# Later marks, sooner routing, and rows mixed by a copy and turned in one pass, in a fused attention and MoE kernel

## The chip, the cores and the metric

The kernel runs on one core of one Trainium2 chip. The metric is the device time of one execution in microseconds; of several executions the median stands.

## What is computed

Three stages follow each other. The first is sliding-window attention over 4 sequences of 576 tokens with 8 heads of 64 (window 64); its output is a matrix x of 2304 rows and 512 columns. The second is a mixture of 8 experts, of which each row takes the two with the highest noisy logits. The third is an MLP with a squared gate.

```python
scores = scale * np.matmul(q, k.transpose(0, 1, 3, 2))
mask = (rel >= 0) & (rel < window)
...
noisy_logits = logits + noise_scale * noise
top2 = np.argpartition(-noisy_logits, 2, axis=1)[:, :2]
...
for e in range(E):
    for k in range(2):
        mask = top2[:, k] == e
        h = np.maximum(x[mask] @ w1[e], 0.0)
        out[mask] += top2_w[mask, k, None] * (h @ w2[e])
...
h = x @ w_in
g = np.where(pos, h, np.where(neg, 0.0, (h + beta) ** 2 / (4.0 * beta)))
return (g @ w_out).astype(np.float32)
```

All data are float32. The kernel forms the large products from a high part (f32r, the value rounded by a copy) and a low part (value minus high part), in three products: high by high, high by low, low by high.

## The kernel before

One function writes the program of all engines in the order of its Python code, and each engine runs its own instructions in that order. SyncE (SP) issues most loads and stores; GpSimd (POOL) issues gathers and scatters by index.

**Attention.** Steps u = 0 to 36 go over half-tiles of 64 rows. Each step issues scores, exponentials and products of several half-tiles at different stages (top, soft, C, Dm, Ex). Dm scales a finished tile of x on VectorE (DVE: rl, its reciprocal, a multiplication) and stores it to x_dram. In the same steps the weights of the first expert come in: load_raw loads a chunk of 128 hidden columns, split_w makes its high part on ScalarE (ACT, L158) and rest_w its low part on DVE (L149); there are seven such chunks (EW) in the attention and one more behind it.

**Routing.** The 18 tiles of x are routed in three groups of 8, 4 and 6 tiles. `route(g)` is a generator: its pieces are some twenty small DVE operations (m, t, uu, w, ny, MAX8 and MAX_INDEX for the two best experts, then ohs, the one-hot marks) and two on ACT (y, L). Then PE counts, for each row, its place among the rows of its expert (L558 to L562, bank<-ohs), and DVE makes marks (ohr, ohe) from which `place` (L634) adds up row numbers on PE. `advance` and `tail`/`more` issue the next pieces; `early` gathers the first three blocks of rows of expert 0, for the unit 0a, before the third group is routed.

**MoE.** Units 0a, 0b, e1 to e6, 7a and 7b are blocks of rows of one expert. For each of eight chunks n, `do_mm1(n)` makes twelve products (L891) and the activation (ACT L899, DVE L902: hall), and `do_mm2` the products with the second weights (L964). In the code do_mm1 runs one chunk ahead of do_mm2.

**The second MLP.** Unit g0 (two blocks of 128 rows) is computed plainly. Units g1 to g4 (four blocks each) use the Strassen-Winograd scheme: for each of eight rounds p, `wino` makes seven products of six matmuls each (L1178) in seven slots j, which alternate between two banks of PSUM; DVE and ACT combine them into cg (L1163, L1168; an eviction frees the bank for the product two slots later). The gate (L1196 to L1206) turns cg into hall, and mm2 matmuls (L964) of an earlier round fill the slots between the products.

During a unit the next one is prepared. Each row of the MoE's output is a weighted sum of two gathered rows y1 and y2 (`prep_mix`: two scalings on ACT, L1043 and L1044, and an addition on POOL, L1045). `xturn` turns it by four transposes on PE (L1236), `xcopy` copies it to xf on ACT (L1242), `xsums` makes four differences xd of quarter matrices (L1255; on POOL, for the first Winograd unit on DVE), and `xsplit` high and low parts. The slot (p, j) of each step is written in the main loop and in the table AT.

## Time and profile before

| | |
|---|---|
| median of 3 runs | 954.07 us (952.11 to 954.48) |
| profiled execution | 953.95 us, span 952.2 us |
| mean granted clock of PE | 0.998 |
| PE busy | 938.4 us |
| DVE busy | 659.5 us |
| ACT busy | 444.3 us |
| POOL busy | 222.1 us |

The span goes from the first to the last instruction of the profiled execution; 1.75 us of its time lie outside. An engine is busy while one of its instructions is under way, whatever the clock of PE is. The granted clock is the share of full speed that the throttle leaves to PE. In a timeline a row gives start and duration in us, engine, line, operation, out<-in with partitions and elements, how many alike are joined in it (x9), and in brackets how long the engine was idle before and what ended that.

### The profile page before, as it was taken

To read this page: it belongs to the slowest core of one execution; us is meant where nothing else is said; L and a number is where in the kernel's file an instruction comes from. 1 tells how busy PE (TensorE), PEld (TensorE's weight loads), DVE (VectorE), ACT (ScalarE), POOL (GpSimd) and SP (SyncE) were. 2 spreads that over 40 slices of the span, in tenths; PEclk is the share of its full clock that TensorE was granted. 3 is DMA by queue.
4 is the path that set the end of the run, shared out by engine and by line. 5 is a ranking of instruction groups with operands and counts; after the bars stand their busy time and mean duration, and the time that the engine had idled before them with its cause. 6 is when DMAs were issued, how large, how long until landed. Compare 5 with 4: busy or idle time off the path is not lost. (4 is left out here: it accounts for less than half of the span.)

```text
span 952.2 us, 18037 instructions
## 1 busy us (share of the span) xinstructions
PE 938.4 (99%) x6779; PEld 832.8 (87%) x6781; DVE 659.5 (69%) x1386; ACT 444.3 (47%) x920; POOL 222.1 (23%) x273
## 2 busy tenths in 40 slices
PE   9999899999999999999999999999999999999998
PEld 6887788988889889889888889988998899899997
DVE  5688665477997968889543377766766777677664
ACT  7897325345565555555432366343334334442221
POOL 4222013133544353354402030013002201300000
PEclk9999999999999999999999999999999999999999
DMA  8884126555888777767626567775586458556521
GB/s 269 289 271 150 50 89 195 187 194 198 285 287 285 256 233 278 258 211 250 244 89 202 201 212 254 256 235 175 177 273 208 149 173 306 174 176 207 188 94 44
DMA packets 91274, 196.95 MB, mean 207 GB/s; under 512 B 7320, under 2 KB 18072, under 8 KB 91184
## 3 DMA queue, kind: packets, MB, share of 16 engines
q1 hardware_dynamic: 83152, 171.68, 54.4%
q0 software_dynamic: 6736, 21.86, 6.4%
q10 hardware_dynamic: 1296, 2.23, 0.6%
q8 instruction: 54, 0.88, 0.4%
q14 instruction: 36, 0.29, 0.1%
HBM read 155.45 MB, written 40.29 MB: 206 GB/s over the span
## 5 line engine op out<-in xcount | busy, mean ns | idle before, releaser
L964 PE MATMUL bank<-wo,hall 128*128 128x512 f32 x864 | 237.6, 394 | 0.0
L964 PE MATMUL bank<-w,hall 128*128 128x512 f32 (+3 forms) x944 | 236.2, 398 | 0.1
L964 PEld LDWEIGHTS bank<-w,hall 128*128 128x128 f32 (+3 forms) x944 | 168.8, 185 | 35.5 <-issue 0.3
L964 PEld LDWEIGHTS bank<-wo,hall 128*128 128x128 f32 x864 | 146.7, 188 | 17.4 <-DVE hall L910 0.2
L899 ACT ACTIVATE hall<-bank 128x288 fp32r<-128x288 f32 (+6 forms) x128 | 54.0, 422 | 219.7 <-PE bank L891 197.3
L891 PE MATMUL bank<-xhie,w 128*128 128x288 f32 (+4 forms) x768 | 122.6, 302 | 0.5 <-DVE hall L902 0.4
L891 PEld LDWEIGHTS bank<-xhie,w 128*128 128x128 f32 x768 | 113.5, 188 | 7.5 <-DVE hall L902 1.3
L902 DVE SCALAR_TENSOR_TENSOR hall<-bank,hall 128x288 fp32r<-128x288 f32 (+7 forms) x168 | 59.9, 390 | 84.3 <-ACT hall L899 76.2
L149 DVE TENSOR_TENSOR w<-raw,w 128x1024 fp32r<-128x1024 f32 (+1 forms) x69 | 82.0, 1188 | 23.7 <-ACT w L158 19.4
L1178 PEld LDWEIGHTS bank<-xb,wi 128*128 128x128 f32 x576 | 80.5, 188 | 10.1 <-DVE cg L1168 1.2
L1202 ACT ACTIVATE hall<-cg 128x512 fp32r<-128x512 f32 x64 | 40.3, 629 | 100.5 <-DVE cg L1200 100.5
L1178 PE MATMUL bank<-xb,wi 128*128 128x256 f32 x576 | 84.7, 282 | 0.6 <-DVE cg L1168 0.3
L1178 PEld LDWEIGHTS bank<-xc,wi 128*128 128x128 f32 x480 | 67.2, 188 | 7.6 <-DVE wg L1163 0.6
L1178 PE MATMUL bank<-xc,wi 128*128 128x256 f32 x480 | 70.2, 281 | 0.2 <-DVE wg L1163 0.2
L1045 POOL TENSOR_TENSOR y<-y,y 128x512 f32<-128x512 f32 x14 | 19.1, 1365 | 217.1 <-ACT y L1044 217.1
L158 ACT ACTIVATE w<-raw 128x1024 fp32r<-128x1024 f32 (+1 forms) x71 | 69.4, 977 | 0.0
L891 PE MATMUL bank<-xloe,w 128*128 128x288 f32 (+4 forms) x384 | 69.1, 302 | 0.0
L204 POOL TENSOR_TENSOR td<-rawd 128x512 f32<-128x512 f32 x32 | 33.3, 1040 | 139.7 <-DVE rawd L202 111.8
L1196 ACT ACTIVATE mg<-cg 128x512 f32<-128x512 f32 x64 | 40.1, 626 | 46.8 <-DVE cg L1168 45.1
L1197 DVE SCALAR_TENSOR_TENSOR cg<-mg,cg 128x512 f32<-128x512 f32 x64 | 46.9, 733 | 18.8 <-ACT mg L1196 18.8
L891 PEld LDWEIGHTS bank<-xloe,w 128*128 128x128 f32 x384 | 58.0, 188 | 0.0
L1206 DVE SCALAR_TENSOR_TENSOR hall<-cg,hall 128x512 fp32r<-128x512 f32 x64 | 45.9, 717 | 9.1 <-ACT hall L1202 8.7
(284 smaller groups left out, 1442.8 us busy)
## 6 DMA issues: line engine op xcount, KB each, us to landing
wi<-w1o SPq DMA_DIRECT2D x56, 1024.0 KB
raw<-wcat SPq DMA_DIRECT2D x64, 512.0 KB
rawd<-wd SPq DMA_DIRECT2D x32, 512.0 KB
w1o<-so SPq DMA_DIRECT2D x64, 256.0 KB
y<-y_dram SPq DMA_DIRECT2D x28, 256.0 KB
vE<-v SPq DMA_DIRECT2D x18, 260.0 KB
x_dram<-x SPq DMA_DIRECT2D x18, 256.0 KB
k<-kT SPq DMA_DIRECT2D x8, 512.0 KB
```

Of the source, the lines that this page charges most:

```text
L149: nc.vector.tensor_tensor(out=w[:, 1, c], in0=t[:, c], in1=w[:, 0, c].bitcast(F32), op=ALU.subtract)
L158: nc.scalar.activation(w[:, 0, c], t[:, c], AF.Copy)
L204: nc.gpsimd.tensor_tensor(out=t, in0=hf, in1=lf, op=ALU.add)
L891: nc.tensor.matmul(ps, lhsT=l[k], rhs=r[:, k, s:s + w], start=(c == 0), stop=(c == len(prods) - 1))
L899: nc.scalar.activation(hh, ps, AF.Relu)
L902: nc.vector.scalar_tensor_tensor(out=t, in0=ps[:, c], scalar=0.0, in1=hh[:, c].bitcast(F32), op0=ALU.max, op1=ALU.subtract)
L964: nc.tensor.matmul(M2[b][0:w], lhsT=h2[:, o:o + w], rhs=r[n], start=(first and a == 0), stop=(last and a == end))
L1178: nc.tensor.matmul(ps, lhsT=w[:, l, k * P:k * P + P], rhs=r[:, m, k, :], start=(c == 0), stop=(c == len(prods) - 1))
L1196: nc.scalar.activation(st["m"], c, AF.Relu, scale=0.5)
L1197: nc.vector.scalar_tensor_tensor(out=c, in0=st["m"], scalar=1.0, in1=c, op0=ALU.min, op1=ALU.subtract)
L1202: nc.scalar.activation(h2[:, 0:T], c, AF.Copy, scale=-1.0)
L1206: nc.vector.scalar_tensor_tensor(out=h2[:, T:2 * T], in0=c, scalar=-1.0, in1=h2[:, 0:T].bitcast(F32), op0=ALU.mult, op1=ALU.subtract)
```

## The change

In the attention and the first unit:

- At step 32 Dm comes ahead of the marks; at step 33 `place` is left out, so the last of the early marks, and `early` with its gathers, come one step later.
- The low part of chunk 4 is made as a whole behind step 34 instead of in two halves in mid-attention; those of chunks 5 and 6 before do_mm1(0) instead of behind do_mm2 of chunks 0 and 2. The eighth load is issued behind the attention.
- `more()` before do_mm1(0) replaces the one behind do_mm2(0), so the pieces of the last routing group come one position sooner.
- The first copy to xhi0a is made by DVE instead of ACT.

In the MoE, both first gathers of the third unit are issued ahead of rank(1), and so ahead of three scatters of POOL.

In the Winograd units g2 to g4 (twelve blocks), `mix_copy` takes the place of `prep_mix`: one scaling on ACT, one scalar_tensor_tensor (STT) on DVE in y2, then a DMA copy of y2 to y1, whose tile is declared f32r, issued by POOL. `xturn` then turns y1 with the f32r identity idr. Turns stand at slots (2,3), (2,5), (3,3), (3,4) instead of (2,1), (2,3), (3,1), (3,3). The four differences xd go to DVE, one each at (3,6), (4,0), (4,6), (5,0), instead of to POOL together at (4,0).

```diff
@@ -703,20 +703,21 @@
 
         if u % 2 == 1 and 0 <= m - 2 < NT:
             logits(m - 2, u)
-        place()
+        if u != NU - 3:
+            place()
         early()
+        if u == NU - 4:
+            Dm(u - 1)
         advance(MARKS[u > NU - 10])
-        if 0 <= u - 1 < NU:
+        if 0 <= u - 1 < NU and u != NU - 4:
             Dm(u - 1)
 
         for c in range(EW):
             for h in range(2):
                 if u == L0 + LS * c + 3 + h:
                     split_w(c, h)
-                if u == L0 + LS * c + 4 + h and c < EW - 2:
+                if u == L0 + LS * c + 4 + h and c < EW - 3:
                     rest_w(c, slice(512 * h, 512 * h + 512))
-            if u == L0 + LS * c + 4 and EW <= c + 2 < NF:
-                load_raw(c + 2)
 
     gat = {}
 
@@ -759,14 +760,21 @@
             nc.tensor.transpose(o[:, k * P:k * P + m], t[0:m, k * P:k * P + P], i[0:m, 0:m])
         tv = TR.rearrange("p (k t) -> p k t", k=4)[:, :, 0:m]
         sl = slice(b * P, b * P + m)
-        nc.scalar.activation(hi[:, :, sl], tv, AF.Copy)
+        if (key, b) == ("0a", 0):
+            nc.vector.tensor_copy(hi[:, :, sl], tv)
+        else:
+            nc.scalar.activation(hi[:, :, sl], tv, AF.Copy)
         nc.vector.tensor_tensor(out=lo[:, :, sl], in0=tv, in1=hi[:, :, sl].bitcast(F32), op=ALU.subtract)
 
     for u in range(NU + 1):
         step(u)
+        if u == NU - 2:
+            rest_w(EW - 3, slice(0, 1024))
         if u == NU - 1:
             xT["0a"] = (wide_x("xhi0a"), wide_x("xlo0a"))
     assert state["first"]
+    for c in range(EW, NF):
+        load_raw(c)
     logits(NT - 2, NU)
     warm(2, Sb[0])
     xpose("0a", 0, P, Sb[0])
@@ -1023,10 +1031,11 @@
             nc.gpsimd.dma_start(out=y, in_=yd)
             y = [y[:, c] for c in range(2)]
         else:
-            y = [pool["sc"].tile([P, DM], F32, tag="s", name=f"y{t}_{c}") for c in range(2)]
+            wide = un is not units[FIRST2] and un is not units[FIRST2 + 1]
+            y = [pool["sc"].tile([P, DM], F32R if wide and c == 0 else F32, tag="s", name=f"y{t}_{c}") for c in range(2)]
             eng = nc.gpsimd if un is units[FIRST2 + 1] else nc.sync
             for c in range(2):
-                eng.dma_start(out=y[c], in_=yd[:, c, :])
+                eng.dma_start(out=y[c].bitcast(F32) if y[c].dtype == F32R else y[c], in_=yd[:, c, :])
         gat[un["key"], b] = (y, t)
 
     def mix_two(un, b):
@@ -1035,6 +1044,15 @@
         yield
         nc.vector.scalar_tensor_tensor(out=y2, in0=y2, scalar=wts[:, t, 1:2], in1=y1, op0=ALU.mult, op1=ALU.add)
         gat[un["key"], b] = y2
+
+    def mix_copy(un, b):
+        (y1, y2), t = gat[un["key"], b]
+        nc.scalar.activation(y2, y2, AF.Copy, scale=wts[:, t, 1:2])
+        yield
+        nc.vector.scalar_tensor_tensor(out=y2, in0=y1.bitcast(F32), scalar=wts[:, t, 0:1], in1=y2, op0=ALU.mult, op1=ALU.add)
+        nc.gpsimd.dma_start(out=y1.bitcast(F32), in_=y2)
+        gat[un["key"], b] = y1
+        yield
 
     def prep_mix(un, b):
         if un["e"] is None:
@@ -1232,8 +1250,9 @@
         t = gat.pop((un["key"], b))
         free = [bank[7]] + [x for x in bank[2:7] if x not in units[ui - 1]["m2"]]
         held[ui, b] = to = free[b % len(free)]
+        o, i = (to.bitcast(F32R), idr) if t.dtype == F32R else (to, idn)
         for k in range(4):
-            nc.tensor.transpose(to[:, k * P:k * P + P], t[:, k * P:k * P + P], idn)
+            nc.tensor.transpose(o[:, k * P:k * P + P], t[:, k * P:k * P + P], i)
 
     def xcopy(ui, b):
         if b == 0:
@@ -1252,7 +1271,7 @@
         b11, b21, b12, b22 = (f[:, i] for i in range(4))
         for i in part:
             out, x, y = ((t1, b12, b11), (t2, b22, t1), (t3, b22, b12), (t4, b21, t2))[i]
-            (nc.vector if d else nc.gpsimd).tensor_tensor(out=out, in0=x, in1=y, op=ALU.subtract)
+            nc.vector.tensor_tensor(out=out, in0=x, in1=y, op=ALU.subtract)
         if 3 in part:
             staged[ui] = (b11, b21, t2, t3, t4, t1, b22)
 
@@ -1283,6 +1302,9 @@
     nload = NF + 2
     n64 = 2 * NF2
     ndec = ndl = 0
+    more()
+    for c in (EW - 2, EW - 1):
+        rest_w(c, slice(0, 1024))
     do_mm1(0)
     ndone = 1
     for s in range(len(seq)):
@@ -1353,16 +1375,13 @@
                 for b in range(nxt["nb"]):
                     prep_xpose(nxt, b, (TR, bank[6])[b])
                 rank(0)
-                prep_gather(units[2], 0)
+                for b in range(2):
+                    prep_gather(units[2], b)
                 rank(1)
         if ui == U7A and f == 2:
             overflow(nc.values_load(cnt_i[0:1, 0:1], min_val=0, max_val=16 * N))
             pool["x4"] = ffn.enter_context(tc.tile_pool(name="x4", bufs=1, reuse_waits="tile"))
         do_mm2(s, ahead_xpose)
-        if s in (0, 2):
-            rest_w(EW - 2 + s // 2, slice(0, 1024))
-        if s == 0:
-            more()
         for _ in range(SPLITS[ui][f] if ui in SPLITS else int(0 < ui < U7A)):
 
             if nsplit == SP:
@@ -1392,7 +1411,9 @@
                 load_out(f + 2)
     assert ndec == n64 and nsplit == nload == N2
 
-    AT = ({(4, 0): (None,), (4, 4): (0,), (4, 5): (1,), (5, 0): (2,), (5, 1): (3,), (5, 3): (4,), (6, 2): (5,), (6, 3): (6,)},
+    mixes = deque()
+    TURN2, SUM2 = [(2, 3), (2, 5), (3, 3), (3, 4)], [(3, 6), (4, 0), (4, 6), (5, 0)]
+    AT = ({(4, 4): (0,), (4, 5): (1,), (5, 0): (2,), (5, 1): (3,), (5, 3): (4,), (6, 2): (5,), (6, 3): (6,)},
           {})
     TURN, COPY = {(3, 0): (0,), (3, 1): (1,), (3, 6): (2,), (4, 0): (3,)}, {(3, 3): (0, 1), (4, 2): (2, 3)}
     g1 = FIRST2 + 1
@@ -1440,10 +1461,15 @@
                     prep_gather(nxt, 2 * p + j)
                 if not late:
                     if 1 <= p < 3 and j in (2, 4):
-                        prep_mix(nxt, 2 * (p - 1) + j // 2 - 1)
-                    if 2 <= p < 4 and j in (1, 3):
-                        xturn(ui + 1, 2 * (p - 2) + j // 2)
-                        xcopy(ui + 1, 2 * (p - 2) + j // 2)
+                        mixes.append(mix_copy(nxt, 2 * (p - 1) + j // 2 - 1))
+                        next(mixes[-1])
+                    if (p, j) in ((1, 6), (2, 0), (2, 6), (3, 0)):
+                        next(mixes.popleft())
+                    if (p, j) in TURN2:
+                        xturn(ui + 1, TURN2.index((p, j)))
+                        xcopy(ui + 1, TURN2.index((p, j)))
+                    if (p, j) in SUM2:
+                        xsums(ui + 1, (SUM2.index((p, j)),))
                 else:
                     for b in TURN.get((p, j), ()):
                         xturn(ui + 1, b)
@@ -1452,7 +1478,7 @@
                     if p == 4 and j > 4:
                         xsums(ui + 1, (0, 1) if j == 5 else (2, 3))
                 for x in AT[late].get((p, j), ()):
-                    xsums(ui + 1) if x is None else xsplit(ui + 1, x)
+                    xsplit(ui + 1, x)
             if j < len(g):
                 g[j]()
             if gen:
```

How the order of instructions moves is shown at three places. The first is DVE at the start of the first MoE unit; m, t, uu, w and ny belong to the last routing group, L149 writes the low part of a weight chunk, and hall<-bank is the activation of a chunk. Before:

```order
L502 TENSOR_SCALAR m_2164<-lgs_1722 128x48
L505 SCALAR_TENSOR_TENSOR t_2166<-m_2164,lgs_1722 128x48
L902 SCALAR_TENSOR_TENSOR hall<-bank_75,hall 128x384
L513 TENSOR_SCALAR uu_2187<-y_2168 128x48
L515 SCALAR_TENSOR_TENSOR w_2186<-uu_2187,y_2168 128x48
L516 RECIPROCAL uu_2187<-uu_2187 128x48
L517 TENSOR_TENSOR m_2164<-m_2164,L_2170 128x48
L519 TENSOR_TENSOR w_2186<-w_2186,uu_2187 128x48
L521 TENSOR_TENSOR w_2186<-m_2164,w_2186 128x48
L523 TENSOR_TENSOR w_2186<-w_2186,nz_sb 128x48
L526 TENSOR_TENSOR ny_2195<-w_2186,lgs_1722 128x48
L149 TENSOR_TENSOR w_1425<-raw_1211,w_1425 128x1024
```

In the changed kernel, behind the same xlo0a:

```order
L502 TENSOR_SCALAR m_2149<-lgs_1718 128x48
L505 SCALAR_TENSOR_TENSOR t_2151<-m_2149,lgs_1718 128x48
L149 TENSOR_TENSOR w_1423<-raw_1211,w_1423 128x1024
L149 TENSOR_TENSOR w_1699<-raw_1425,w_1699 128x1024
L910 SCALAR_TENSOR_TENSOR hall<-bank_74,hall 128x384
L513 TENSOR_SCALAR uu_2174<-y_2153 128x48
L515 SCALAR_TENSOR_TENSOR w_2173<-uu_2174,y_2153 128x48
L516 RECIPROCAL uu_2174<-uu_2174 128x48
L517 TENSOR_TENSOR m_2149<-m_2149,L_2155 128x48
L519 TENSOR_TENSOR w_2173<-w_2173,uu_2174 128x48
L521 TENSOR_TENSOR w_2173<-m_2149,w_2173 128x48
L523 TENSOR_TENSOR w_2173<-w_2173,nz_sb 128x48
```

Both L149 now stand ahead of the first hall, the pieces uu to ny ahead of the second, and no L149 stands between ny and MAX.

The second place is DVE in the first Winograd unit, from the end of one round (wg, cg) to the start of the gate in the next. Before:

```order
L1206 SCALAR_TENSOR_TENSOR hall<-cg_3_0_7619,hall 128x512
L1168 SCALAR_TENSOR_TENSOR cg_4_1_7724<-bank_74,tg_4_7790 128x256
L1163 TENSOR_TENSOR wg_4_7819<-bank_74,ug_4_7769 128x256
L1168 SCALAR_TENSOR_TENSOR cg_4_0_7723<-bank_73,wg_4_7819 128x256
L1197 SCALAR_TENSOR_TENSOR cg_4_1_7724<-mg_4_1_7835,cg_4_1_7724 128x512
L1200 SCALAR_TENSOR_TENSOR cg_4_1_7724<-mg_4_1_7835,cg_4_1_7724 128x512
```

Changed, where y_1 is the mixed row block and y_0 the other:

```order
L1181 TENSOR_TENSOR wg_4_7814<-bank_74,ug_4_7755 128x256
L1052 SCALAR_TENSOR_TENSOR y_1_7612<-y_0_7611,wts,y_1_7612 128x512
L1186 SCALAR_TENSOR_TENSOR cg_4_0_7722<-bank_73,wg_4_7814 128x256
L1052 SCALAR_TENSOR_TENSOR y_1_7632<-y_0_7631,wts,y_1_7632 128x512
L1215 SCALAR_TENSOR_TENSOR cg_4_1_7723<-mg_4_1_7834,cg_4_1_7723 128x512
L1218 SCALAR_TENSOR_TENSOR cg_4_1_7723<-mg_4_1_7834,cg_4_1_7723 128x512
L1186 SCALAR_TENSOR_TENSOR cg_5_0_7837<-bank_73,sg_5_7846 128x256
```

Two STT now stand between the last evictions of the round and the gate's operations; one round and two rounds later two xd subtractions stand at the same places.

The third place is PE in round 3 of that unit, where the third and the fourth block of the next unit are turned. Before:

```order
L1178 MATMUL bank_74<-xb_7151,wi_6343 128x256 x6
L964 MATMUL bank_2138<-wo_6770,hall 128x512 x3
L1236 MATMUL bank_78<-idn,y_1_7613 128x128 x4
L1178 MATMUL bank_73<-xb_7152,wi_6502 128x256 x6
L964 MATMUL bank_77<-wo_6770,hall 128x512 x3
L1178 MATMUL bank_74<-xb_7153,wi_6502 128x256 x6
L964 MATMUL bank_2139<-wo_6770,hall 128x512 x3
L964 MATMUL bank_75<-wo_6770,hall 128x512
L1236 MATMUL bank_76<-idn,y_1_7633 128x128 x4
L1178 MATMUL bank_73<-xb_7154,wi_6502 128x256 x6
L964 MATMUL bank_75<-wo_6770,hall 128x512 x2
```

Changed:

```order
L972 MATMUL bank_2138<-wo_6769,hall 128x512 x3
L972 MATMUL bank_75<-wo_6769,hall 128x512
L1255 MATMUL bank_78<-idr,y_0_7611 128x128 x4
L1196 MATMUL bank_73<-xb_7153,wi_6501 128x256 x6
L972 MATMUL bank_75<-wo_6769,hall 128x512 x2
L972 MATMUL bank_2137<-wo_6769,hall 128x512
L1255 MATMUL bank_76<-idr,y_0_7631 128x128 x4
L1196 MATMUL bank_74<-xa_7228,wi_6501 128x256 x6
L972 MATMUL bank_2137<-wo_6769,hall 128x512 x2
```

The turns have moved two slots and one slot back, read y_0 instead of y_1, and use idr instead of idn.

## Rows read from the trace of the kernel before

**Rows 1.** The page, busy time of each engine: us (share) xinstructions.
```profile
PE 938.4 (99%) x6779; PEld 832.8 (87%) x6781; DVE 659.5 (69%) x1386; ACT 444.3 (47%) x920; POOL 222.1 (23%) x273
```

**Rows 2.** Windows: busy time of PE, PEld, DVE, ACT, POOL, PEclk, DMA share, GB/s.
```profile
115.00:120.00 5.00, 5.00 (x25) 4.30 (x24) 2.88 (x14) 1.01 (x3) 0.00 (x0) 0.77 0.01 3
```

**Rows 3.** Timeline of PE, DVE and ACT, 102 to 120 us: start, us, work.
```profile
102.98 0.69 DVE L763 TENSOR_TENSOR xlo0a<-bank,xhi0a 128x512 fp32r<-128x512 f32 x1 [0.97 <-ACT xhi0a L762]
...
105.93 0.56 DVE L902 SCALAR_TENSOR_TENSOR hall<-bank,hall 128x384 fp32r<-128x384 f32 x1 [2.26 <-ACT hall L899]
...
108.48 0.18 DVE L513 TENSOR_SCALAR uu<-y 128x48 f32<-128x48 f32 x1
...
110.28 1.22 DVE L149 TENSOR_TENSOR w<-raw,w 128x1024 fp32r<-128x1024 f32 x1
...
110.78 0.86 PE L891 MATMUL bank<-xlo0a,w 128*128 128x384 f32 x4
111.42 0.50 DVE L530 MAX8 mx<-ny 128x8 f32<-128x8 f32 x6
...
112.06 1.05 ACT L158 ACTIVATE w<-raw 128x1024 fp32r<-128x1024 f32 x1
...
113.53 0.18 PE L558 MATMUL bank<-ohs,tri 128*128 128x48 bf16 x1 [1.89 <-DVE ohs L543]
...
113.70 3.89 PE L964 MATMUL bank<-w,hall 128*128 128x512 f32 x9
...
115.47 0.25 DVE L567 TENSOR_TENSOR o<-o,bank 128x96 f32<-128x96 f32 x1
...
117.73 0.26 DVE L593 TENSOR_SCALAR ohe<-io,rf 128x145 f16<-128x145 f16 x1
...
119.66 0.42 PE L634 MATMUL bank<-ohe,ohr 128*128 128x145 f16 x4
...
119.88 2.33 PE L964 MATMUL bank<-w,hall 128*128 128x512 f32 x9
```

**Rows 4.** Timeline of PE in a Winograd unit, 632 to 660 us.
```profile
639.76 0.60 PE L1236 MATMUL bank<-idn,y 128*128 128x128 f32 x4
640.12 0.96 PE L1178 MATMUL bank<-xb,wi 128*128 128x256 f32 x6
...
641.61 0.87 PE L1178 MATMUL bank<-xa,wi 128*128 128x256 f32 x6
...
646.30 0.87 PE L1178 MATMUL bank<-xb,wi 128*128 128x256 f32 x6
...
653.05 0.87 PE L1178 MATMUL bank<-xa,wi 128*128 128x256 f32 x6
...
658.52 0.98 PE L1178 MATMUL bank<-xb,wi 128*128 128x256 f32 x6 [0.16 <-DVE wg L1163]
```

**Rows 5.** Timeline of DVE in the same unit, 642 to 660 us.
```profile
649.13 0.42 DVE L1168 SCALAR_TENSOR_TENSOR cg<-bank,sg 128x256 f32<-128x256 f32 x1 [1.74 <-PE bank L1178]
...
652.98 1.38 DVE L1197 SCALAR_TENSOR_TENSOR cg<-mg,cg 128x512 f32<-128x512 f32 x1 [2.09 <-ACT mg L1196]
```

**Rows 6.** Instructions of line L1255: min/median/max ns, first and last start.
```profile
L1255 POOL TENSOR_TENSOR xd<-xf x6: 1307/1534/1755, 652.5 to 829.0; 128x512 f32<-128x512 f32 x6
...
L1255 DVE TENSOR_TENSOR xlos<-xhis x2: 683/683/683, 589.0 to 590.3; 128x512 f32<-128x512 f32 x2
```

**Rows 7.** Timeline of PE in an MoE unit, 200 to 215 us.
```profile
208.60 0.46 PE L759 MATMUL bank<-idr,xge 128*128 128x128 f32 x4
208.90 2.78 PE L964 MATMUL bank<-w,hall 128*128 128x512 f32 x11
```

**Rows 8.** Timeline of POOL, 126 to 129 us.
```profile
128.19 1.02 POOL L863 DMA_INDIRECT xg0b<-x_dram,src_i  x1 [0.30 <-issue]
```

**Rows 9.** Windows of 1 us, the columns of rows 2.
```profile
131.00:132.00 1.00, 1.00 (x7) 0.96 (x6) 0.87 (x7) 0.00 (x0) 0.00 (x0) 1.00 0.05 16
```

**Rows 10.** Timeline of POOL, 560 to 570 us.
```profile
568.02 2.24 POOL L1023 DMA_DIRECT2D y<-y_dram  x3 [4.74 <-DMA y_dram<-y7b,rank_i]
```

## The prediction

> **What bounds the kernel now.** I began with the page: TensorE (PE) is busy for 99% of the span [rows 1], so only two things can shorten this kernel: less work on PE, or PE work that runs at its undisturbed length. A busy share of 99% hides the second kind, because a matmul that starts late or runs at a low clock still counts as busy. So I read next where PE's clock is below full, then the timeline of PE and VectorE (DVE) around that place, and then PE's spacing from product to product in the Winograd units, with what DVE and GpSimd (POOL) did in a slow stretch.
>
> Two places stand out. In the first unit of the MoE the granted clock falls to 0.77 of full speed in 115–120 us [rows 2], that is, part of that stretch ran at the lower of the two levels, 1.2 instead of 2.4 GHz. Just ahead of it PE stood 1.89 us waiting for ohs, the one-hot marks of the last routing group, and the next nine mm2 matmuls took 3.89 us, where nine of the same shape took 2.33 a little later [rows 3]. In the Winograd units the same run of three slots takes 641.61 to 646.30 = 4.69 us undisturbed and 653.05 to 658.52 = 5.47 us one round later [rows 4]. In that later stretch DVE's L1197 took 1.38 us [rows 5]; POOL was then in its xd subtractions, which start at 652.5, take 1.3 to 1.8 us each, and come twelve times in all, four for each of three units [rows 6].
>
> **Part 1, the routing.** ohs is late because of what DVE does before it. In the new order DVE has, from the end of the last xlo0a at 102.98 + 0.69 = 103.67: m and t (two operations like uu, 0.2 each: 0.4), two whole L149 (2 × 1.22 = 2.44), hall(0) and hall(1) (2 × 0.56 = 1.1), uu to ny (108.48 to 110.28: 1.8), and MAX8 to ohs (111.42 to 113.53, where PE is released: 2.1) [rows 3]. The sum is 7.84, so ohs comes at 111.51. PE would get there at 113.53 − 1.89 = 111.64. The wait is gone, by a margin of 0.13 only. ACT makes y and L during the two L149, which cover it. hall(0) now ends near 103.67 + 0.4 + 2.44 + 0.56 = 107.07 rather than at 105.93 + 0.56 = 106.49 [rows 3]; mm2 of that chunk stands behind twelve products of the second chunk in PE's order, so I take 0, at most 0.6.
>
> Without the wait, I expect no fall of the clock either, since what stood ahead of it was that idle time. So the gain is 1.89 + (3.89 − 2.33) = 3.45 up to the next thing that PE needs, the marks for place. For these DVE goes on with the eighth chunk's L149, which needs ACT's L158 (112.06 + 1.05 = 113.11) and so ends at 114.33 whatever DVE saves; then from 115.47 to 117.73 + 0.26 = 2.52 of small operations give the marks at 114.33 + 2.52 = 116.85 [rows 3]. PE would be at place at 119.66 − 3.45 = 116.21, so 0.64 of the wait comes back there. **Term: −2.8.** Bounds: −3.45 if those marks are in time; −1.2 if the short wait at place lowers the clock again for as long as before (2.8 − 1.56).
>
> The other moves of this part I take at 0. Chunk 4's low part leaves DVE in mid-attention and comes back at its end as one operation (1.22, as the whole L149 [rows 3]), where DVE waits for PE and ACT anyway; bounds ± 1.2. The later marks and gathers of the first unit are covered by the attention's last matmuls; the eighth load, now behind the x stores on SP's queue, could meet those gathers: bound +1.9, as long as one gather's transfer (below), 0 taken, since its reader L158 is 10 us off.
>
> **Part 2, the gathers of the third unit.** One of them goes ahead of three scatters on POOL. No wait of PE here names POOL: 0.
>
> **Part 3, xd leaves POOL.** Twelve POOL subtractions become DVE operations. DVE has made the same subtraction (L1255 for the first Winograd unit) in 0.68 us [rows 6]. What it takes away is the slowed DVE: 5.47 − 4.69 = 0.78 for three slots, and the next product takes 0.98 instead of 0.87, another 0.11 [rows 4]; 0.89 for each of the three units. **Term: −2.7.** What it adds, two operations a round at slots 6 and 0 in four rounds of each unit (the one-pass mixing first, xd after), is 2 × 0.68 = 1.4 between evictions; it goes into the gap that DVE has before the first eviction of the next round, 1.74 us, in which it waits for PE [rows 5]. So I take 0 for it. Bounds of the whole: −0.9 (only one unit is slowed as in the rows) and −2.7.
>
> The Trainium skill has this rule on its page "SBUF — State Buffer", section "Who interferes with whom": a DVE operation with two SBUF inputs and a GpSimd operation that reads SBUF slow each other. The trace agrees, with 1.38 for L1197 beside POOL. It names no loss of PE's time.
>
> **Part 4, mixing and turning.** ACT loses one of two scalings, POOL its addition (not on PE's path before). DVE gets one STT per block, the same shape as the subtraction, 0.7, with the gap above. PE turns twelve blocks of four transposes with idr as f32r instead of idn as f32. From the first transpose to the next product PE took 640.12 − 639.76 = 0.36 in f32 [rows 4], and 208.90 − 208.60 = 0.30 for the same four turns in f32r in an MoE unit [rows 7]. **Term: 12 × 0.06 = −0.7**; bounds 0 and −1.4 (twice that).
>
> **The sum.** −2.8 − 2.7 − 0.7 = −6.2 from the profiled execution's 953.95 is 947.75; the median of the runs is 0.12 above that execution, so about **947.8**. With every term at its bad end (−1.2, −0.9, 0) it is 952.0, at its good end (−3.45, −2.7, −1.4) 946.5.
>
> **Rivals.**
> *One pass costs a quarter.* If a turn in one pass took a quarter of its 0.36, each block would save 0.27, 3.2 in all, and the time would be 945.3. Rows 7 speak against it: the f32r turn is there at 0.30. The Trainium skill's page "FP8 and Floating Point Precision", section "TensorE Precision Notes", puts true FP32 at four passes of the array, which is the rule behind this rival; the rows of f32r turns don't show it for four short transposes.
>
> *The copies come late.* Between STT and turn stands now a DMA copy issued by POOL. A round is 653.05 − 641.61 = 11.44, a slot of seven 1.63 [rows 4]. Blocks 0, 2 and 3 of a unit have three slots between STT and turn, 4.9 us, block 1 four, 6.5. A gather's issue took 1.02 on POOL [rows 8], and all its data were there by about 131.05, 1.9 after the issue [rows 9]: 2.9 in all, in time. The slowest landing I found is 4.74 after the issue, for the last scatter of y7b [rows 10]: 5.8 in all, 0.9 late. Then PE waits at blocks 0 and 2 (block 3 gains what block 2 loses), 6 × 0.9 = 5.2, and the time is 953.0; halfway 950.4.
>
> *Slower: DVE holds the copies' descriptors back.* If POOL's writing of a copy's descriptors has to wait while DVE runs operations with two SBUF inputs, and each copy (issued right behind an STT, ahead of L1197 and L1200) meets two of these, 2 × 0.68 = 1.4 on top of 5.8 is 7.2, 2.3 late; six such waits make 13.5 and the time 961.3. It decides from a landing of 4.9 + 6.2 / 6 = 5.9 us on: above that, the waits eat the whole gain. Against it: the issue of rows 8 ran at 1.02 while DVE was busy with its small operations. [...] No run so far shows how long such a hold lasts here.
>
> *DVE becomes the bound.* If each of 24 added operations delays an eviction that PE waits for by half its 0.68, the loss is 8.2: 956.0. The gap of 1.74 speaks against it.
>
> **How the numbers follow.** Forecast 0.62 (own range 945.5 to 951), quarter 0.06, late copies 0.16 (949 to 953), held descriptors 0.10, DVE bound 0.06. No change that can be measured is within 0.3%, 951.2 to 956.9. Faster: 0.62 + 0.06 + 0.11 of the late copies = 0.79; same: 0.05 of the late copies and 0.04 of the last two = 0.09; slower 0.12. The range of 944.0 to 952.5 takes in the quarter with all good ends (953.95 − 3.45 − 2.7 − 3.2 = 944.6) and the late copies nearly to their worst, and leaves out the last two rivals.
>
> **What would show it.** Right: no wait for ohs at L558's new line near 111.6, nine mm2 matmuls behind it in about 2.3, the clock at 1.00 in 110–120; L1215 (the old L1197) at 0.7 in the round after the last turn, and three slots at 4.7 there; four f32r turns in 0.30 to the next product. Wrong: idle PE before the turns with the copy as releaser; a PE wait for wg, cg or hall in rounds 1 to 5 of a Winograd unit; a clock below 1.00 behind place.

## The result, and the profile after

The changed kernel is slower: 958.91 us in the median of 6 runs (956.21 to 959.10) against 952.23 of 6 runs of the kernel before, a ratio of 1.0056 with a 95% interval of 1.0039 to 1.0073. (The ratio is worked out over all runs, 5.3 us; the medians alone are 6.7 us apart. The 954.07 that the forecast started from is the median of the first three of the six runs of before.) Forecast were 947.8 us and a ratio of about 0.993. The profiled execution took 959.1 us, 5.15 more than that of before.

From the page of the changed kernel, the busy times and the head of the chain that ended last. PE is about as busy as before (939.8 and 938.4 us [rows 1]), in a longer span, and the chain now holds 3% of DMA, the transfer y<-y, which the kernel before did not have:

```profile
span 957.4 us, 18043 instructions
...
PE 939.8 (98%) x6781; PEld 834.9 (87%) x6781; DVE 666.9 (70%) x1410; ACT 437.0 (46%) x907; POOL 192.3 (20%) x261
...
PE 36%; issue 7%; DMA 3%; DVE 1%; POOL 0%; ACT 0%; POOLq 0%
```

Where the time went is seen by comparing the start of the same instruction in both executions. This table is worked out from the timelines of PE; a number is how much later than in the profiled execution of before that instruction starts. Each column less the one to its left is what the stage between them cost.

| kernel | first product of unit 0a (before: 103.00) | mm2 of chunk 3 (119.88) | near the end of the MoE (552.4) | behind the first turned unit (690.0) | second (780.4) | third (864.9) |
|---|---|---|---|---|---|---|
| changed | +4.63 | +2.21 | +1.02 | +1.67 | +2.93 | +5.16 |
| e1 routing alone | −0.09 | −3.08 | −4.32 | −4.29 | −4.33 | −4.31 |
| e2 load sooner | +3.74 | +1.13 | −0.30 | +0.63 | +1.93 | +2.67 |
| e3 turns later | +4.30 | +1.62 | +0.40 | −0.78 | −1.99 | −3.20 |
| e4 no copy | +0.49 | −2.50 | −3.74 | −4.62 | −5.57 | −6.48 |
| e5 place back | +0.10 | −2.90 | −4.21 | −3.53 | −0.64 | +0.01 |
| e6 marks first | +3.31 | +1.73 | +0.37 | +1.17 | +4.25 | +4.91 |
| e7 all mended | −0.46 | −3.46 | −4.67 | −5.86 | −7.07 | −8.29 |
| e8 copies by ACT | +4.32 | +2.36 | +1.07 | +1.61 | +1.93 | +2.50 |
| e9 STT sooner | +3.55 | +1.45 | +2.66 | +2.20 | +1.55 | +0.53 |
| e10 f32 turns | +1.09 | −1.91 | −1.03 | −1.94 | −2.86 | −3.79 |
| e12 store by POOL | +0.06 | −2.92 | −4.19 | −3.11 | −1.67 | −1.03 |

The row of the changed kernel tells the case: 4.63 us are lost before unit 0a, 2.4 won in its first chunks, 1.2 more by the end of the MoE, and 4.1 lost again while the three units of the second MLP are turned. The 1.2 come at two places, near 154.6 and 470 us, where PE stood 0.48 and 0.26 us in the profiled execution of before; e1 and e4 have them too. All runs here have the routing part, so whether they are a gain of it or a mark of that one execution is not shown. (That execution is 1.7 us above the median of its 6 runs, so rows of this table look up to that much better than the medians below.)

**The attention's end.** The timeline of PE of the changed kernel around the start of unit 0a:

```profile
103.17 0.75 PE L760 MATMUL bank<-idr,xg0a 128*128 128x128 f32 x4 [3.37 <-DMA xg0a<-x_dram,src_i]
...
107.63 2.24 PE L899 MATMUL bank<-xhi0a,w 128*128 128x384 f32 x8
...
116.67 0.20 PE L558 MATMUL bank<-ohs,tri 128*128 128x48 bf16 x1
...
116.87 2.29 PE L972 MATMUL bank<-w,hall 128*128 128x512 f32 x9
...
122.06 0.22 PE L634 MATMUL bank<-ohe,ohr 128*128 128x145 f16 x1 [0.17 <-DVE ohe L593]
122.08 2.34 PE L972 MATMUL bank<-w,hall 128*128 128x512 f32 x9
```

PE stood 3.37 us for the second early gather, and its clock fell in that wait. In windows of 1 us of the changed kernel, PEclk third from the end, it is 0.50 from 102 to 108 us:

```profile
101.00:102.00 1.00, 0.00 (x0) 0.00 (x0) 0.00 (x0) 0.00 (x0) 0.00 (x0) 0.91 0.93 332
102.00:103.00 1.00, 0.00 (x0) 0.00 (x0) 0.00 (x0) 0.00 (x0) 0.00 (x0) 0.50 0.96 377
...
107.00:108.00 1.00, 1.00 (x4) 0.50 (x3) 0.84 (x3) 0.09 (x1) 0.00 (x0) 0.50 0.00 0
```

The same two places in the kernel before, where the clock was 1.00:

```profile
99.74 0.53 PE L759 MATMUL bank<-idr,xg0a 128*128 128x128 f32 x4
...
103.00 1.68 PE L891 MATMUL bank<-xhi0a,w 128*128 128x384 f32 x8
```

So of the 4.63 us 3.43 are lost at the second turn (103.17 against 99.74), and 1.20 from there to the first product at the low clock. The first eight products then take 2.24 instead of 1.68, another 0.56 that the table counts against the gain of the first chunks.

Behind that the forecast of the routing came true: L558 waits for nothing, where it waited 1.89, the nine mm2 matmuls take 2.29 instead of 3.89 [rows 3], and 0.17 of waiting is left at place. The windows of the changed kernel show the full clock there (1.00), where it was 0.77 [rows 2]:

```profile
110.00:115.00 5.00, 5.00 (x28) 4.61 (x27) 4.13 (x28) 0.98 (x2) 0.00 (x0) 1.00 0.00 0
115.00:120.00 5.00, 5.00 (x33) 4.49 (x32) 3.41 (x12) 1.44 (x2) 0.00 (x0) 1.00 0.00 0
```

How the gathers were issued is in the timeline of DVE, POOL and SP of the changed kernel:

```profile
94.03 0.16 DVE L476 SCALAR_TENSOR_TENSOR src_i<-few 128x3 int32<-128x3 f32 x1
...
94.50 1.24 POOL L733 DMA_INDIRECT xg0a<-x_dram,src_i  x1 [4.00 <-DVE src_i L476]
...
95.62 3.36 SPq L412 DMA_DIRECT2D x_dram<-x  x2
...
96.03 1.54 POOL L733 DMA_INDIRECT xg0a<-x_dram,src_i  x1 [0.30 <-issue]
```

The indices are ready at 94.2. SP's store of tile 16 goes out at 95.62 (the row joins two stores, the other at 98.66), 0.4 us ahead of the second gather, and the gather lands 7.1 us after its issue, near 103.1. In the kernel before that store went out at 95.75, behind the second gather (93.98) and the third (95.27).

**The copies.** The timeline of PE in the units of the second MLP; the rows at 642.08, 729.58 and 817.63 are the first turn of each unit, those at 818.01 and 820.20 the two products behind the third, and from 655.52 to 660.27 go the three slots of [rows 4]:

```profile
642.08 0.54 PE L1255 MATMUL bank<-idr,y 128*128 128x128 f32 x4 [1.56 <-DMA y<-y]
...
655.52 0.95 PE L1196 MATMUL bank<-xa,wi 128*128 128x256 f32 x6
...
660.27 0.87 PE L1196 MATMUL bank<-xb,wi 128*128 128x256 f32 x6
...
729.58 0.53 PE L1255 MATMUL bank<-idr,y 128*128 128x128 f32 x4 [1.66 <-DMA y<-y]
...
817.63 0.54 PE L1255 MATMUL bank<-idr,y 128*128 128x128 f32 x4 [1.66 <-DMA y<-y]
818.01 1.11 PE L1196 MATMUL bank<-xa,wi 128*128 128x256 f32 x6
...
820.20 1.48 PE L1196 MATMUL bank<-xa,wi 128*128 128x256 f32 x6
```

In each unit PE waits for the first copy (and in the second 0.34 us for the fourth too), and in the third the clock falls behind the wait: the products take 1.11 and 1.48 instead of 0.87. Windows of that place, PEclk third from the end:

```profile
816.00:818.00 2.00, 0.37 (x4) 0.37 (x5) 0.00 (x0) 0.00 (x0) 0.00 (x0) 1.00 0.66 267
818.00:820.00 2.00, 2.00 (x11) 1.81 (x11) 0.64 (x2) 1.72 (x3) 0.00 (x0) 0.65 0.00 0
820.00:822.00 2.00, 2.00 (x9) 1.81 (x9) 1.26 (x4) 0.63 (x1) 0.00 (x0) 0.50 0.66 221
```

0.50 is the lower of the two levels, 1.2 instead of 2.4 GHz; it came after 1.66 us of an idle PE. The differences on DVE do what was forecast: the three slots take 660.27 − 655.52 = 4.75 us, not 5.47 [rows 4], and L1215 (the old L1197, 1.38 in [rows 5]) is back at 0.69, with xd among the evictions:

```profile
655.08 0.69 DVE L1215 SCALAR_TENSOR_TENSOR cg<-mg,cg 128x512 f32<-128x512 f32 x1 [1.95 <-ACT mg L1214]
...
658.81 0.68 DVE L1274 TENSOR_TENSOR xd<-xf 128x512 f32<-128x512 f32 x1
```

Why the copy is late stands in the view of the DMA queues. These are the transfers that were issued in short windows of the changed kernel, with the KB of each and the us from issue to landing: SP's weight load at 635.16, the copy of block 0 at 635.83, the copy of block 2 at 648.80, and that of block 3 at 649.88.

```profile
wi<-w1o SPq DMA_DIRECT2D x1, 1024.0 KB, 6.2
...
y<-y POOLq DMA_DIRECT2D x1, 256.0 KB, 6.2
...
y<-y POOLq DMA_DIRECT2D x1, 256.0 KB, 2.3
...
y<-y POOLq DMA_DIRECT2D x1, 256.0 KB, 5.2
```

The copy behind the load of 1 MB takes as long as that load. Block 2's takes 2.3: the load ahead of it was issued 5.4 us sooner and landed 0.2 us behind the copy's issue. Block 3's was issued together with the next load, at 649.88, and took 5.2 (5.2 to 5.7 in the three units). What the queues moved from 636.4 to 639.5, and then from 639.5 to 642.2 (packets, MB, share of 16 engines), shows that the copies did not even begin before most of the load was through (block 2's copy moved its first packet 1.1 us after its issue, block 0's after 4.1):

```profile
q1 hardware_dynamic: 360, 0.74, 94.9%
...
q0 software_dynamic: 158, 0.52, 47.7%
q1 hardware_dynamic: 151, 0.28, 29.4%
```

### The profile page after: what moved, and what is told of

Read it like the earlier page. It is cut to its first block, busy times and chain, and to the rows that moved or that the text cites. A ratio compares the mean times of both kernels' runs of the same rounds, so it can differ in the third digit from the quotient of the medians.

```text
span 957.4 us, 18043 instructions
## 1 busy us (share of the span) xinstructions
PE 939.8 (98%) x6781; PEld 834.9 (87%) x6781; DVE 666.9 (70%) x1410; ACT 437.0 (46%) x907; POOL 192.3 (20%) x261
## 5 line engine op out<-in xcount | busy, mean ns | idle before, releaser
L899 PE MATMUL bank<-xhie,w 128*128 128x288 f32 (+4 forms) x768 | 122.6, 302 | 0.3 <-DVE hall L910 0.2
L899 PEld LDWEIGHTS bank<-xhie,w 128*128 128x128 f32 x768 | 113.6, 188 | 7.1 <-DVE hall L910 1.3
L149 DVE TENSOR_TENSOR w<-raw,w 128x1024 fp32r<-128x1024 f32 (+1 forms) x68 | 81.7, 1203 | 24.0 <-ACT w L158 22.2
L899 PE MATMUL bank<-xloe,w 128*128 128x288 f32 (+4 forms) x384 | 69.1, 302 | 0.0
L1215 DVE SCALAR_TENSOR_TENSOR cg<-mg,cg 128x512 f32<-128x512 f32 x64 | 43.8, 685 | 23.5 <-ACT mg L1214 23.5
L899 PEld LDWEIGHTS bank<-xloe,w 128*128 128x128 f32 x384 | 58.1, 188 | 0.0
L1053 POOL DMA_DIRECT2D y<-y x12 | 6.5, 538 | 249.0 <-DVE cg L1186 170.7
L1224 DVE SCALAR_TENSOR_TENSOR hall<-cg,hall 128x512 fp32r<-128x512 f32 x64 | 43.9, 686 | 7.4 <-ACT hall L1220 7.0
```

Of the source, the lines that this page charges most:

```text
L149: nc.vector.tensor_tensor(out=w[:, 1, c], in0=t[:, c], in1=w[:, 0, c].bitcast(F32), op=ALU.subtract)
L899: nc.tensor.matmul(ps, lhsT=l[k], rhs=r[:, k, s:s + w], start=(c == 0), stop=(c == len(prods) - 1))
L1215: nc.vector.scalar_tensor_tensor(out=c, in0=st["m"], scalar=1.0, in1=c, op0=ALU.min, op1=ALU.subtract)
L1224: nc.vector.scalar_tensor_tensor(out=h2[:, T:2 * T], in0=c, scalar=-1.0, in1=h2[:, 0:T].bitcast(F32), op0=ALU.mult, op1=ALU.subtract)
```

## The experiments

Two theories stood against each other. Theory W, later Q: both losses are transfers that land late because another one went out just ahead of them. Rivals: the start a step later by itself (L), and POOL's descriptors held back by DVE (D). All ratios are to the kernel before on the same chip, with their 95% intervals. "Changed" is the changed kernel, at 1.0056.

**e1: routing alone**, in the kernel before.

```diff
+    more()
+    for c in (EW - 2, EW - 1):
+        rest_w(c, slice(0, 1024))
     do_mm1(0)
...
-        if s in (0, 2):
-            rest_w(EW - 2 + s // 2, slice(0, 1024))
-        if s == 0:
-            more()
```

> The kernel before with one part alone: the pieces of the last routing group and the low parts of chunks 5 and 6 ahead of do_mm1(0). Theory (the gain of the routing is real and stands by itself): ohs is in time, the nine mm2 matmuls behind it take about 2.3 us instead of 3.89, and the time is 2.2 to 2.8 us under the kernel before, ratio about 0.9974. Rival (in the changed kernel DVE was in time only because the late gathers held PE back by 4.6 us): the wait for ohs stays at 0.5 us or more, the clock falls again, and the time is at most 1 us under the kernel before.

949.79 us, 0.9978 (0.9969 to 0.9986): 2.1 us faster by the ratio, 2.3 by the medians. In its PE timeline L558 waits for nothing at 111.38, against the 111.64 of the forecast, and the matmuls behind take 2.29:

```profile
111.38 0.20 PE L558 MATMUL bank<-ohs,tri 128*128 128x48 bf16 x1
...
111.57 2.29 PE L964 MATMUL bank<-w,hall 128*128 128x512 f32 x9
```

So the gain is real without the late gathers: 2.99 us from the first product to mm2 of chunk 3 in the table.

**e2: the eighth load sooner.** Changed, with chunk 4's low part in two halves in mid-attention and load_raw(7) at step 25.

```diff
-                if u == L0 + LS * c + 4 + h and c < EW - 3:
+                if u == L0 + LS * c + 4 + h and c < EW - 2:
                     rest_w(c, slice(512 * h, 512 * h + 512))
+            if u == L0 + LS * c + 4 and EW <= c + 2 < NF:
+                load_raw(c + 2)
...
-        if u == NU - 2:
-            rest_w(EW - 3, slice(0, 1024))
...
-    for c in range(EW, NF):
-        load_raw(c)
```

> The changed kernel with the eighth load back at step 25 and the low part of chunk 4 back in two halves in mid-attention; marks, place and early gathers stay one step later. Theory W (the gathers of the first unit are late because the eighth load of 512 KB shares the DMA engines with them): the wait of 3.37 us at the second turn of gathered rows falls under 1 us, the first product of unit 0a starts at about 104.5 instead of 107.6, and the time is some 3 us under the changed kernel. Rival L (they are late because their indices are ready 2 us later): the wait stays at 2 us or more and the time within 1.5 us of the changed kernel.

956.61 us, 1.0056 (1.0035 to 1.0077). The wait is nearly all there, so the eighth load is not the main cause; unit 0a starts 0.9 us sooner than in the changed kernel, which is the most that it and chunk 4's low part can cost:

```profile
102.28 0.75 PE L762 MATMUL bank<-idr,xg0a 128*128 128x128 f32 x4 [2.91 <-DMA xg0a<-x_dram,src_i]
```

Its POOL timeline has the issue of the second gather at 0.98 us, where the changed kernel has 1.54:

```profile
95.46 0.98 POOL L735 DMA_INDIRECT xg0a<-x_dram,src_i  x1 [0.30 <-issue]
```

**e3: turns two slots later.** Changed, with

```diff
-    TURN2, SUM2 = [(2, 3), (2, 5), (3, 3), (3, 4)], [(3, 6), (4, 0), (4, 6), (5, 0)]
+    TURN2, SUM2 = [(2, 5), (3, 0), (3, 5), (3, 6)], [(4, 0), (4, 2), (4, 6), (5, 0)]
```

> The changed kernel with the turns of the copied rows two slots (3.3 us) later, and the four differences at slots (4,0), (4,2), (4,6), (5,0). Theory W (the copies land some 6 us after their issue, behind a weight load of 1 MB, whatever the turns do): landings stay at up to 6.3 us, the waits of 1.6 to 1.7 us before the first turn of each unit are gone, the clock in 814 to 825 us is 1.00, and the time is 4.5 to 6 us under the changed kernel. Rival (PE's order gives the copies their pace, or the differences on DVE now delay evictions): new waits of PE for cg or wg in rounds 4 and 5, and a gain under 2.5 us.

950.23 us, 0.9974 (0.9964 to 0.9984). PE waits for no copy any more and the clock stays at 1.00 in the three units, while the first copy still lands 6.3 us after its issue:

```profile
y<-y POOLq DMA_DIRECT2D x1, 256.0 KB, 6.3
```

The three units now win 3.6 us (+0.40 to −3.20 in the table) where the changed kernel lost 4.1. By the ratios the gain is 7.8 us, more than the 4.5 to 6 that theory W said; the 3.6 of the three units are near the 3.4 of parts 3 and 4. PE has no new wait for wg or cg, here or in the changed kernel, so the differences on DVE delay nothing.

**e4: no copy.** The kernel before with the routing of e1, the gathers of part 2 and the differences on DVE; POOL's additions and the turns in f32 stay.

```diff
-            (nc.vector if d else nc.gpsimd).tensor_tensor(out=out, in0=x, in1=y, op=ALU.subtract)
+            nc.vector.tensor_tensor(out=out, in0=x, in1=y, op=ALU.subtract)
...
+    SUM2 = [(3, 6), (4, 0), (4, 6), (5, 0)]
...
+                    if (p, j) in SUM2:
+                        xsums(ui + 1, (SUM2.index((p, j)),))
```

> The kernel before with three parts of the change: the routing of run e1, the gathers of the third unit ahead of the scatters, and the four differences on DVE at the slots of the change; mixing on ACT and POOL, turns in f32 and the attention stay as before. Theory W (the losses are all in the copies and in the attention's end): 2.4 for the routing, 0.7 for the gathers, 3 x 0.8 for the differences, 5.5 us under the kernel before, ratio about 0.9942. Rival (the differences on DVE gain only because the one-pass mixing took POOL's additions away too): 3 us or less, ratio 0.997 or more.

947.59 us, 0.9952 (0.9939 to 0.9964), 4.6 us faster, where 5.5 were expected and the rival said 3 or less. Each unit wins 0.9 us (−3.74, −4.62, −5.57, −6.48), with POOL's additions still there. The gathers' order, from which 0.7 was expected, gives nothing of its own: the steps of e1, which has not got it, are as large up to the end of the MoE.

**e5: place back.** Changed, with place and Dm as before; eighth load and chunk 4 as changed.

```diff
-        if u != NU - 3:
-            place()
+        place()
         early()
-        if u == NU - 4:
-            Dm(u - 1)
         advance(MARKS[u > NU - 10])
-        if 0 <= u - 1 < NU and u != NU - 4:
+        if 0 <= u - 1 < NU:
             Dm(u - 1)
```

> The changed kernel with place back in step 33 and Dm back behind the marks in step 32, so the early gathers start one step sooner as before; the eighth load stays behind the attention and chunk 4's low part at its end. Theory L (the gathers are late because they start a step later, among the last x stores): the wait of 3.37 us at the second turn is under 0.5 us, unit 0a starts its products some 4 us sooner, and the time is 3.5 to 4.5 us under the changed kernel, about 954.8. Rival W (the eighth load and the held descriptors by themselves): the load starts after the gathers' issue in any case, so the wait stays over 1.5 us and the gain is under 2.5 us.

953.96 us, 1.0014 (1.0002 to 1.0027), 4.0 us under the changed kernel by the ratios. Unit 0a starts 4.5 us sooner than in the changed kernel, and the second gather lands 4.3 us after its issue; at the third turn 0.20 us of waiting is left:

```profile
101.88 0.54 PE L757 MATMUL bank<-idr,xg0a 128*128 128x128 f32 x4 [0.20 <-DMA xg0a<-x_dram,src_i]
```

**e6: marks first.** Changed, with Dm of half-tile 31 alone back behind the marks (e5's edit without its first three lines, those on place).

> The changed kernel with Dm of half-tile 31 back behind the marks of step 32 alone; place and the early gathers stay one step later. Theory L (the later start): the wait at the second turn stays over 2 us, and the time is within 1.5 us of the changed kernel. Rival S (the x store that now goes out sooner, just ahead of the first gather, is what stretches the gathers): the second gather lands within 6.5 us of its indices as in run e1, where it took 6.05, the wait is under 1.5 us and the time some 2 us lower.

957.73 us, 1.0042 (1.0027 to 1.0057), within 1.5 us of the changed kernel. The wait is 1.84, the gather lands 5.4 us after its issue: between the two expectations, so this run alone decides nothing. The store of tile 16 is still issued 0.4 us ahead of the second gather (96.16 and 96.57), as in the changed kernel; why the gather lands 1.7 us sooner than there is open.

```profile
102.02 0.56 PE L758 MATMUL bank<-idr,xg0a 128*128 128x128 f32 x4 [1.84 <-DMA xg0a<-x_dram,src_i]
```

**e7: all mended.** Changed, with the edits of e2, e3 and e5, and the first xhi0a copy on ACT again.

> The changed kernel with its whole attention part undone (place, Dm, the eighth load, chunk 4, the first xhi0a copy) and the turns two slots later as in run e3; routing, gathers of the third unit, mixing by a copy, one-pass turns and differences on DVE stay. If the two losses are separate, the 4.3 us of the attention's end come off run e3: about 946.0, ratio 0.9935, 1 to 2 us under run e4, which has no copies. If the gain of run e3 hangs on its late start, 948 or more.

946.97 us, 0.9942 (0.9925 to 0.9959), 5.5 us faster than before, the lowest ratio of the study, though its interval overlaps e4's. It lies between the two expectations, nearer the first. The table decides: the three units win 3.62 us here (−4.67 to −8.29) and 3.60 in e3, with a start 5 us earlier, so the losses are separate.

**e8: copies by ACT.** Changed, with

```diff
-        nc.gpsimd.dma_start(out=y1.bitcast(F32), in_=y2)
+        nc.scalar.dma_start(out=y1.bitcast(F32), in_=y2)
```

> The changed kernel with the twelve copies issued from ScalarE's queue instead of POOL's; all else as changed. Theory W (the copies lie behind a weight load of 1 MB on the DMA engines): the first copy of a unit still lands 5.5 us or more after its issue, the waits of 1.6 us stay, and the time is within 1.5 us of the changed kernel or above, since ACT now waits for the STT. Rival D (POOL's descriptor writing is held back by DVE's operations with two SBUF inputs): landing in under 3.5 us, no waits at the turns, 4 to 5 us under the changed kernel.

955.01 us, 1.0016 (1.0000 to 1.0031). The first copy, issued 0.04 us behind the load, lands no sooner, 6.8 us after its issue beside 7.0 for the load:

```profile
wi<-w1o SPq DMA_DIRECT2D x1, 1024.0 KB, 7.0
y<-y ACTq DMA_DIRECT2D x1, 256.0 KB, 6.8
```

PE still waits 1.3 to 1.5 us in each unit, so POOL and its descriptors are not the cause. The time is 3.8 us under the changed kernel by the ratios, more than the 1.5 that theory W allowed; in its profiled execution the clock fell in none of the three units, the third cost 0.6 us instead of 2.2, and blocks 2 and 3 landed in 2.3 and 2.5.

**e9: STT sooner.** Changed, with

```diff
-                    if (p, j) in ((1, 6), (2, 0), (2, 6), (3, 0)):
+                    if (p, j) in ((1, 5), (1, 6), (2, 6), (3, 0)):
```

> The changed kernel with the STT of blocks 0 and 1 of each unit one slot (1.6 us) sooner, at (1,5) and (1,6), so that the first copy is issued ahead of the weight load that SP issues at about 635; turns stay where the change has them. Theory W (a copy issued ahead of that load lands in 2.3 to 3 us, one behind it in 6): block 0's copy lands some 3 us after its issue, the waits of 1.6 us before the first turn of each unit are gone, and the time is 4 to 6 us under the changed kernel. Rival (a copy takes 6 us there whatever lies ahead): it lands 1.6 us sooner than in the changed kernel at most, a wait of up to 0.4 us stays. An STT at slot 5 may delay an eviction by up to 0.7 us in each unit.

953.91 us, 1.0000 (0.9991 to 1.0010), 5.3 us under the changed kernel by the ratios, within the 4 to 6 of theory W. The first copy, issued at 635.51, ahead of the load at 636.82, is through by 638.2: in the window 635.5 to 638.2 the queue of POOL moved

```profile
q0 software_dynamic: 80, 0.26, 25.3%
```

which is one copy of 256 KB. PE waits for it in no unit, with the turns where the change has them. The second copy, now behind the load, is 0.25 us late for its turn in the first unit; the 0.32 us of the second unit are the fourth copy's, for which the changed kernel waits there as well. This run loses 2 us elsewhere, told below.

**e10: f32 turns.** e7 without the copies.

```diff
-        nc.gpsimd.dma_start(out=y1.bitcast(F32), in_=y2)
-        gat[un["key"], b] = y1
+        gat[un["key"], b] = y2
```

> Run e7 without the twelve copies: mixing by one scaling on ACT and the STT on DVE, turns of the mixed rows in f32 at the same slots. By the rows of f32 and f32r turns (0.36 and 0.30 us to the next product) 12 x 0.06 = 0.7 us over run e7, which the medians hardly tell and the traces do. Rival (one pass costs a quarter of f32): 3.2 us over run e7.

950.28 us, 0.9965 (0.9953 to 0.9977). In the three units it wins 2.8 us (−1.03 to −3.79) where e7 wins 3.6: the copies and f32r turns are worth about 0.85, not 3.2. The rest of the difference to e7 lies ahead of those units.

**e11: store later.** Changed, with the store of tile 16 written in the code behind that of tile 17.

> The changed kernel with the x_dram store of tile 16 held back until tile 17 is ready, so that no store goes out between the first and the second early gather; place, the early gathers, the eighth load and chunk 4's low part stay as changed. Theory Q (a transfer issued just behind another one on the DMA engines lands after it, at the attention's end as with the copies): the second gather lands 6 to 6.5 us after its indices instead of 8.9, the wait of 3.37 us at the second turn falls under 1.2 us, and the time is 1.5 to 3 us under the changed kernel; a new wait of up to 1 us may come at the third turn, since both stores and the eighth load now go out together. Rival L (the step later alone): landing stays at 8 us or more and the wait over 2 us.

957.69 us, 1.0038 (1.0017 to 1.0058). The store still went out at 96.3, since SP issues it as soon as its data are ready and has nothing between that would hold it. The run says nothing on the question; with the order unchanged its second gather landed 6.5 us after its issue.

**e12: store by POOL.** Changed, with

```diff
-        nc.sync.dma_start(out=x_dram[P * i:P * i + P, :], in_=x.rearrange("p h d -> p (h d)"))
+        eng = nc.gpsimd if i == NT - 2 else nc.sync
+        eng.dma_start(out=x_dram[P * i:P * i + P, :], in_=x.rearrange("p h d -> p (h d)"))
```

> The changed kernel with the x_dram store of tile 16 issued by POOL behind the three early gathers instead of by SP; everything else as changed, the eighth load too. This is what run e11 was meant to do: there the store stayed where it was, since SP had nothing between that held it back. Theory Q (the second gather is late because the store of tile 16 goes out just ahead of it): the second gather lands 6 to 6.5 us after its indices instead of 8.9, the wait of 3.37 us at the second turn falls under 1.2 us, and the time is 1.5 to 3 us under the changed kernel. Rival L (the step later by itself): landing stays at 8 us or more, the wait over 2 us, the time within 1 us.

955.63 us, 1.0032 (1.0018 to 1.0045), about 2.3 us under the changed kernel by the ratios, whose intervals leave some 2 us of play. The second gather lands 4.8 us after its issue instead of 7.1 (6.7 after its indices, just over the 6.5 that theory Q allowed), and the wait falls from 3.37 to 1.27, with the clock at 1.00 behind it:

```profile
100.45 0.54 PE L761 MATMUL bank<-idr,xg0a 128*128 128x128 f32 x4 [1.27 <-DMA xg0a<-x_dram,src_i]
```

So in these two executions the store ahead of it is some two thirds of the wait; that the later start is the rest is argued, not tested by itself. All runs with landing times fit: the second gather lands 5.4 to 7.1 us after its issue in the six with that store 0.4 us ahead of it (changed, e2, e3, e6, e8, e11), and 4.2 to 4.9 in the five with the store behind it (e1, e4, e5, e7, e12).

## Why the prediction was wrong

**Part 1, the routing, −2.8: right.** 2.42 us in the changed kernel and 2.99 in e1, by the mechanism given, clock included; the 0.57 between the two are the first products at the low clock, 2.24 instead of 1.68. By its ratio e1 is 2.1 us faster.

**The step that failed first** is the sentence "The later marks and gathers of the first unit are covered by the attention's last matmuls", taken at 0; the bound of +1.9 beside it was for the eighth load. It cost 4.6 us up to the first product: a wait of 3.37, and 1.2 at the clock of 0.50 that followed it, a fall that I had priced at place and not here. I counted the step by which the gathers start later and not what they then meet: the store of tile 16 now goes out ahead of the second gather, not behind it. e5 undoes that and the loss is gone; e12 moves the store alone, and in its profiled execution (2.6 us under the median of its runs) unit 0a is back at +0.06; by the ratios it regains 2.3 of the 4.0 us that e5 does. The transfer that I did name, the eighth load, is not the main cause: with it in place e5 waits 0.20, without it e2 waits 2.91. My range left out that +1.9 and the +1.2 of chunk 4; with both, its bad end is 955.1 and still too low.

**The second that failed** is the slack of the copies. I held 2.9 us for likely and 5.8 for the worst; the first two copies of a unit take 5.9 to 6.3, the third 2.3, the fourth 5.2 to 5.7. The 2.9 came from a gather on quiet DMA engines [rows 8, 9], but each unit's first copy is issued 0.7 us behind a weight load of 1 MB, which I never looked up: its issue is tied to the same round as the STT, so the meeting happens in every unit. The rival had the right place and was priced at 5.2 us in all. The waits add up to just that (1.56 + 1.66 + 0.34 + 1.66 = 5.22), but by luck: three of 1.6 for block 0 and one of 0.34, not six of 0.9 for blocks 0 and 2. The units went from the −3.4 that I forecast for them (parts 3 and 4) to +4.1, 7.5 us: these waits, and for most of the rest the low clock in the third unit.

**Part 3, −2.7: right**, 0.9 a unit in e4. **Part 4, −0.7: right**, 0.30 to the next product in f32r and 0.36 in f32, 0.85 in all by e7 and e10; the rival of the quarter falls. **Part 2, 0: right** as far as e1 and e4 can tell. *DVE becomes the bound* falls: in the changed kernel's second MLP no wait of PE for DVE is longer than 0.28 us, and that one stands at the same place before (0.27). With both failed steps undone, e7 comes to −5.5 by its ratio where the sum was −6.2.

**Held descriptors:** an issue on POOL is stretched in the changed kernel, but at another place and for 0.56 us: the second gather's takes 1.54 us beside chunk 4's L149 at 95.51 (1.22 us, two SBUF inputs) and 0.98 in e2, where no such operation runs then. The copies' issue took 0.54 each, that of block 0 (635.83) with an STT (635.51, 0.74 us) and L1215 (636.17) of DVE beside it, so that rival was not what made them late. The Trainium skill (page "SBUF — State Buffer", section "A bandwidth-pool intuition that's wrong (but worth ruling out)") tells of a DMA of POOL whose descriptors wait while DVE runs a tensor_copy. That is another operation than these, and beside the two-input ones the copies' issue was not stretched.

The Trainium skill, page "DMA: Bandwidth & Descriptors", section "Issuing engines are not separate DMA queues", says that transfers issued by ACT, SP or POOL run on the same 16 engines, whichever issued them. By that, e8 could not help, and the trace agrees: 6.8 us from ACT's queue, 6.2 from POOL's. The same page, section "Queues, rings and completion order", has each engine go round between the queues that have work. By that, a copy behind a load would move from the start, at its share; the rows differ: not one packet of the copies from 636.4 to 639.5 while the load ran at 95%. What holds their first packet back is not shown by any run here.

## What to carry to other kernels

Before putting a DMA copy between two engines, look up which loads are issued within a microsecond of it, and take its time from a copy that stands behind such a load, not from one on quiet engines. A step that is moved later also changes which other transfers it stands behind; list them in order of issue on all queues, before and after. What the copy saved here (0.85 us) was far less than one wait for it (1.6 us, or 3.4 with a fallen clock: +2.2 for the third unit here, −1.2 in e3), while moving two-input work off POOL paid 0.9 us a unit at no price.

## What the runs showed of the hardware that was not expected

The order of issue decides: 256 KB issued 1.3 us ahead of 1 MB landed within 2.7 us (e9), 0.7 us behind it in 6.2.

A wait of PE of 1.6 us sometimes costs twice: in the changed kernel the clock stayed at 1.00 behind such a wait in two units and fell to 0.50 in the third, in e5 it fell in the second (+2.9 us there in the table). Behind the waits of 1.84 to 3.37 us at the attention's end it fell in all seven runs that have one (changed, e2, e3, e6, e8, e9, e11), behind the 1.27 of e12 not. Which wait of 1.6 us it strikes is open.

In e10 and e9 PE stood 2.0 and 2.1 us near 154 and 157 us, at the second turn of a gathered block of unit e1. In e10 ACT's L899 sat idle for 4.92 us, and the products that it waits for had ended 3.5 us before it started:

```profile
154.21 0.54 PE L759 MATMUL bank<-idr,xge 128*128 128x128 f32 x4 [2.04 <-DVE xloe L763]
```

```profile
152.56 0.38 ACT L899 ACTIVATE hall<-bank 128x256 fp32r<-128x256 f32 x1 [4.92 <-PE bank L891]
```

The order of instructions there is that of e7, which has no such wait. In the profiled execution of before ACT stood 3.36 us and PE 0.48 at the same place (154.58). These three are also the only executions whose pages give no landing times of DMAs (some tenth of those records is missing), so what ACT waited for can't be read. The cause is open; it makes profiled executions differ by up to 2 us.
